# Dividing attention probabilities before the transposes in a fused block-attention and gMLP kernel

## The chip, the core and the metric

The kernel runs on one core of one Trainium2 chip. Five engines matter: TensorE (PE: matmuls and transposes into PSUM; PEld is its weight load), VectorE (DVE), ScalarE (ACT), GpSimd (POOL) and SyncE (SP), whose queue issues the kernel's loads and stores. Each engine works through its own queue in order and waits on semaphores. The metric is device microseconds of one execution; a time below is the median of several executions, and one further execution was profiled.

## The reference, cut to what matters

```python
# attention: q, k, v are (8, 8, 576, 64) f32; the mask lets block i see blocks j <= i, blocks of 64
scores = q @ k.T / 8;  scores = where(mask, scores, -1e9)
attn = exp(scores - scores.max(-1));  attn = attn / (attn.sum(-1) + 1e-9)
x = (attn @ v) -> (8, 576, 512)          # heads side by side
# gMLP: d_ff = 1024
h = gelu_tanh(x @ w_in);  u, v = halves of h
v_n = (v - mean) / sqrt(var + 1e-6) * g_ln
gated = u * (w_sg @ v_n + b_sg[:, None])
out = x + gated @ w_out
```

## The kernel before, in words

**Precision.** Matrix products whose operands must keep float32 accuracy are split: an operand is copied into a rounded high part (`fp32r`) and the rest is subtracted into a low part, and three products (high·high, low·high, high·low) are accumulated. So q and k, x, the normalised v, the gated values and all weights each need a copy and a subtraction. `w_in` and `w_out` arrive as float64 and are turned into float32 by one ScalarE pass and three DVE passes per 128x256 chunk (`from_f64`), ahead of their split.

**Attention, in slots.** A pair is two heads of one batch element; there are 32, four per batch element. `slot(n)` finishes pair n (its values, class `Values`) while it starts pair n+1 (its scores, class `Scores`). The 576 query rows stand in five tiles of rows: tile 0 has 64, tiles 1 to 4 have 128 each, and tile i needs 64+128·i key columns. On PE a slot runs `turn0` (transposes of the first 128 probability columns of tiles 4, 3, 2, 1, for head a=0, then 1), step 1 (scores of tile 4, first half, and tile 1), `av0`, `turn2`, step 2 (tile 4, second half), `turn1`, `turn_first`, step 3 (tiles 3 and 0), `av2`, step 4 (tile 2), `av1`, `av00`. Behind each step DVE takes the maximum (`maximum`, a custom instruction and a one-element read of its accumulator), and ScalarE the exponential with the row sum as an accumulator (`exponent`).

**Normalisation before.** Probabilities are not divided. `inverse` (line 438) forms 1/(sum+1e-9) on DVE and GpSimd spreads it into `rx`, 128x640; `turn_sums` (line 456) sends `rx` through PE with five transposes per slot; `normalise` (line 487) copies the accumulated output to `x` on ScalarE and multiplies it by the transposed sums on DVE. `x` is stored to DRAM (`spill`) and `split` into `xh` and `xl` for the feed-forward part.

**Feed-forward, in holes.** After four slots a batch element's `v_part` (5 pieces of PE work), `u_part` (8), the previous element's `o_part` (8) and its own `s_part` (8) are queued. Each slot has seven places called `hole`, and the strings in `PLAN` (in `FIRST` for slots 4 to 7) tell how many pieces each place takes. In slots 0 to 3 the queue is empty, so these slots hold attention alone. LayerNorm runs as small pieces (`moments`, `centre`, `scale`) taken from a list at fixed places; `WS` tells how many weight chunks a slot asks for.

**What sets the order.** PE instructions keep program order (`PIN = "P"`). For the other engines and for SP's queue the compiler's scheduler chooses the order: it takes instructions as its own model of time makes them ready, so code order there is only a starting point. Once chosen, each engine's order is fixed.

## Time and profile before

| | |
|---|---|
| time, median of 3 | 837.57 us (836.84 to 838.59) |
| profiled execution | 838.82 us, span of its instructions 836.9 us |
| mean granted TensorE clock | 0.966 |
| bytes moved | 65.67 MB, mean 78 GB/s |
| chain that ended last | PE 63%, DVE 20%, ACT 6%, DMA 5%, POOL 3%, issue 3% |

Busy time of one engine is a share of the whole span; what limits the kernel differs by stage: a start of some 26 us, attention alone up to 77 us, the first batch element with feed-forward work up to about 190 us, a regular part with one batch element per 97 to 99 us up to 767 us, and feed-forward alone to the end. A row of a timeline gives start, duration, what ran, and in brackets the idle time of the engine before it and what ended it. A row of the windows gives each engine's busy time (and instructions) in one stretch. A row of the groups gives total busy time, mean ns of one instruction and the idle time ahead of them.

### The profile page before, as it was taken

To read this page: it belongs to the slowest core of one execution; us is meant where nothing else is said; L and a number is where in the kernel's file an instruction comes from. 1 tells how busy PE (TensorE), PEld (TensorE's weight loads), DVE (VectorE), ACT (ScalarE), POOL (GpSimd) and SP (SyncE) were. 2 spreads that over 40 slices of the span, in tenths; PEclk is the share of its full clock that TensorE was granted. 3 is DMA by queue.
4 is the path that set the end of the run, shared out by engine and by line. 5 is a ranking of instruction groups with operands and counts; after the bars stand their busy time and mean duration, and the time that the engine had idled before them with its cause. 6 is when DMAs were issued, how large, how long until landed. Compare 5 with 4: busy or idle time off the path is not lost.

```text
span 836.9 us, 15898 instructions
## 1 busy us (share of the span) xinstructions
PE 788.5 (94%) x5926; PEld 649.0 (78%) x5926; DVE 531.6 (64%) x1504; ACT 424.4 (51%) x1124; POOL 352.7 (42%) x402
## 2 busy tenths in 40 slices
PE   5798992999999999999999999999999999999998
PEld 3466871878878888887887878788787878878998
DVE  6876474894865658564776747766586647753432
ACT  4776663656654367344653357642764446531400
POOL 5445158461543417432372513634164323713251
PEclk8799995999999999999999999999999999999999
DMA  7233205221122112310133101321123201230031
GB/s 251 77 114 115 85 18 159 80 61 57 44 86 99 58 58 72 126 59 30 58 108 120 58 28 31 126 101 57 58 71 122 77 16 57 75 112 29 1 114 71
DMA packets 46912, 65.67 MB, mean 78 GB/s; under 512 B 4082, under 2 KB 22514, under 8 KB 46836
## 3 DMA queue, kind: packets, MB, share of 16 engines
q1 hardware_dynamic: 46836, 64.67, 24.1%
q8 instruction: 46, 0.75, 0.4%
q14 instruction: 30, 0.25, 0.1%
HBM read 45.78 MB, written 18.87 MB: 77 GB/s over the span
## 4 chain that ended last, share of the span: by engine, by line
PE 63%; DVE 20%; ACT 6%; DMA 5%; POOL 3%; issue 3%; SPq 0%; DVEq 0%; ACTq 0%; POOLq 0%
PE accs L86 14%; PE accv L86 13%; PE acco L86 9%; PE ob L86 9%; PE s L86 7%; PE pb L89 3%; DVE prob L99 3%; DVE bs L99 3%; DVE vh L99 2%; DVE vv L99 2%; PE pa L89 2%; PE accu L86 2%; ACT prob L99 2%; PE pc L89 2%; DMA xr<-spill 2%
## 5 line engine op out<-in xcount | busy, mean ns | idle before, releaser
L99 ACT ACTIVATE prob<-prob,negm 128x448 f32<-128x448 f32 (+3 forms) x320 | 178.0, 558 | 157.8 <-DVE negm L99 154.1
L99 DVE CUSTOM_DVE_ANT_0 prob<-s,mask 128x288 f32<-128x288 f32 (+2 forms) x320 | 119.4, 421 | 37.2 <-PE s L86 36.5
L99 POOL TENSOR_TENSOR q_l<-q_f,q_h 128x576 fp32r<-128x576 f32 x31 | 44.2, 1425 | 196.1 <-PE s L86 158.3
L86 PE MATMUL ob<-pt,v_f 128*64 128x512 f32 (+4 forms) x640 | 115.3, 452 | 0.0
L99 POOL TENSOR_TENSOR gl<-u,gh 128x288 fp32r<-128x288 f32 x64 | 52.3, 824 | 105.1 <-DVE gh L99 72.9
L86 PE MATMUL accs<-ws_h,vh 128*128 128x288 f32 x256 | 79.8, 312 | 8.9 <-DVE vh L99 8.9
L86 PE MATMUL s<-k_h,q_h 64*128 64x288 f32 (+1 forms) x372 | 86.7, 351 | 1.2 <-DVE negm L99 1.2
L86 PE MATMUL accs<-ws_h,vl 128*128 128x288 f32 x256 | 76.8, 300 | 6.1 <-POOL vl L99 6.1
L86 PE MATMUL accu<-xh,wi_h 128*128 128x288 f32 x256 | 78.6, 307 | 1.3 <-ACT wi_h L99 1.3
L86 PE MATMUL acco<-gh,wo_h 128*128 128x288 f32 x256 | 79.8, 312 | 0.0
L86 PE MATMUL acco<-gl,wo_h 128*128 128x288 f32 x256 | 76.5, 299 | 0.0
L86 PE MATMUL acco<-gh,wo_l 128*128 128x288 f32 x256 | 76.4, 299 | 0.0
L86 PE MATMUL accs<-ws_l,vh 128*128 128x288 f32 x256 | 76.2, 298 | 0.0
L86 PE MATMUL accu<-xh,wi_l 128*128 128x288 f32 x256 | 75.4, 295 | 0.3 <-POOL wi_l L99 0.3
L86 PE MATMUL accu<-xl,wi_h 128*128 128x288 f32 x256 | 75.6, 295 | 0.0
L86 PE MATMUL s<-k_l,q_h 64*128 64x288 f32 (+1 forms) x372 | 72.2, 298 | 0.0
L86 PEld LDWEIGHTS ob<-pt,v_f 128*64 128x64 f32 x640 | 40.1, 139 | 40.9 <-issue 20.8
L86 PE MATMUL accv<-wi_h,xh 128*128 128x512 f32 x160 | 66.2, 414 | 0.7 <-POOL xh L99 0.7
L99 DVE TENSOR_TENSOR xr<-acco,xr 128x288 f32<-128x288 f32 x64 | 29.0, 454 | 59.2 <-PE acco L86 21.7
L86 PE MATMUL s<-k_h,q_l 64*128 64x288 f32 (+1 forms) x372 | 66.1, 293 | 0.0
L99 DVE TENSOR_TENSOR u<-accs,u 128x288 f32<-128x288 f32 x64 | 28.7, 448 | 57.6 <-PE accs L86 57.6
L86 PEld LDWEIGHTS s<-k_h,q_h 64*128 64x128 f32 x372 | 49.6, 180 | 18.2 <-issue 12.4
(106 smaller groups left out, 2109.9 us busy)
## 6 DMA issues: line engine op xcount, KB each, us to landing
spill<-x SPq DMA_DIRECT2D x32, 288.0 KB, 3.0
xr<-spill SPq DMA_DIRECT2D x32, 288.0 KB, 3.1
out_T<-xr SPq DMA_DIRECT2D x32, 288.0 KB, 2.4
q_f<-in_qT SPq DMA_DIRECT2D x31, 288.0 KB, 3.1
k_f<-in_kT SPq DMA_DIRECT2D x31, 288.0 KB, 3.4
v_f<-in_v SPq DMA_DIRECT2D x32, 256.0 KB, 3.3
raw<-in_w_in SPq DMA_DIRECT2D x16, 256.0 KB, 5.0
raw<-in_w_out SPq DMA_DIRECT2D x8, 256.0 KB, 4.3
```

Of the source, the lines that this page charges most:

```text
L86: return pin(nc.tensor.matmul(*a, **k), "P")
L89: return pin(nc.tensor.transpose(out, in_, identity), "P")
L99: return lambda *a, **k: pin(f(*a, **k), self.letter)
```

## The change

The probabilities themselves are divided. `divide` runs behind the exponentials: two small DVE instructions form 1/(sum+1e-9) for one or two tiles, then tile 4 (576 columns) is multiplied on DVE and tile 3 (448) on GpSimd, by a two-tensor instruction whose second operand is the broadcast reciprocal, and tiles 0 to 2 on ScalarE with the reciprocal as scale. `inverse`, `turn_sums` and the two multiplications of `normalise` go, and with them the five transposes per slot. In LayerNorm, `scale` no longer uses GpSimd: ScalarE writes the scaled high part, one DVE instruction the low part. q and k are loaded into one tile and rounded by one DVE copy of 1152 columns. `WS` asks for the weights of `v_part` alone in the first four slots, `FIRST` moves the first s pieces to the end of slot 6, the start-up keeps DVE and ScalarE in program order, `xr` is loaded one piece ahead, and `split` of a batch element's first two pairs waits until its second slot ends.

```diff
-            q_f = sp.tile([P, S], F32, tag="q_f", name="q_f", bufs=1)
-            k_f = sp.tile([P, S], F32, tag="k_f", name="k_f", bufs=1)
+            t = sp.tile([P, 2, S], F32, tag="qk_f", name="qk_f", bufs=1)
+            q_f, k_f = t[:, 0, :], t[:, 1, :]
...
     def split_qk(n):
+        t = qk[n]
+        hi = sp.tile([P, 2, S], F32R, tag="qk_h", name="qk_h", bufs=1)
+        lo = sp.tile([P, 2, S], F32R, tag="qk_l", name="qk_l", bufs=1)
+        V.tensor_copy(hi, t)
+        for i in (1, 0):
+            G.tensor_tensor(lo[:, i, :], t[:, i, :], hi[:, i, :].bitcast(F32), op=ALU.subtract)
...
-        A.activation(m.bitcast(F32), hi.bitcast(F32), AF.Abs, scale=2.0**-112)
+        A.mul(m.bitcast(F32), hi.bitcast(F32), 2.0**-112)
...
+        def divide(self, *tiles):
+            i0, i1 = min(tiles), max(tiles)
+            ts = slice(i0, i1 + 1, max(i1 - i0, 1))
+            V.tensor_tensor(self.ri[:, ts, :], self.sm[:, ts, :], tiny[:, ts, :], op=ALU.add)
+            V.reciprocal(self.ri[:, ts, :], self.ri[:, ts, :])
+            for i in tiles:
+                r, e = slice(0, QN[i]), EXT[i]
+                for a in (0, 1):
+                    x, c = self.prob[a][i][r, :e], self.ri[r, i, a : a + 1]
+                    if i < 3:
+                        A.mul(x, x, c)
+                    else:
+                        engine = V if i == 4 else G
+                        engine.tensor_tensor(x, x, c.broadcast_to([QN[i], e]), op=ALU.mult)
...
-            turn(self.t4[:, 128:256], self.rx[:, 0, :], ident)
-            t = self.rp = pbank("pe")
-            for i in range(1, NT):
-                turn(t[:, (i - 1) * P : i * P], self.rx[:, i, :], ident)
...
-            V.tensor_tensor(x[:, BLK:], self.rp, x[:, BLK:], op=ALU.mult)
-            V.tensor_tensor(x[:, :BLK], self.t4[:, 128:192], x[:, :BLK], op=ALU.mult)
...
-            paced(G.tensor_tensor(x, x, r.broadcast_to([rows, DH]), op=ALU.mult), "G")
             if st < NT - 1:
                 hi, lo = vn[st] = page(F32R, DH, "vh"), page(F32R, DH, "vl")
-                V.tensor_copy(hi, x)
-                G.tensor_tensor(lo, x, hi.bitcast(F32), op=ALU.subtract)
+                A.mul(hi, x, r)
...
+            paced(V.scalar_tensor_tensor(
+                lo, x, r, hi.bitcast(F32), op0=ALU.mult, op1=ALU.subtract
+            ), "V")
...
+        def reload(mo):
+            if mo < NC:
+                x_r[mo] = page(F32, S, "xr")
+                SP.dma_start(x_r[mo], spill.pop((b, mo)))
...
-    WS = [2, 2, 2, 2, 4, 3, 4, 4, 3]
+    WS = [2, 2, 2, 1, 10, 3, 3, 3, 2]
...
-    FIRST = ["1111111", "1111111", "1010101", "1010010"]
+    FIRST = ["1111111", "1111110", "0000011", "1111110"]
...
         if nx:
             nx.exponents(4)
+            nx.divide(4, 1)
...
             nx.exponents(3, 0)
+            nx.divide(3, 0)
             nx.step4()
         va.av1()
         va.av00()
-        va.turn_sums()
         if nx:
             nx.exponents(2)
+            nx.divide(2)
...
+    kept.update("VA")
     sc = Scores(0)
...
+    kept.difference_update("VA")
```

Three places of the instruction order bear on what follows. A number behind a tile's name is that of its buffer.

GpSimd, in slot 1, the second of the slots with attention alone (`q_l`, `k_l`, `qk_l`: low parts of q and k of the pair after next; `rx`: spread reciprocals; `xh`, `xl`: split of the finished pair's output; `prob_3`: tile 3 of the two heads of the next pair). Before:

```order
L99 TENSOR_TENSOR q_l<-q_f,q_h 128x576
L99 TENSOR_TENSOR k_l<-k_f,k_h 128x576
L99 MEMSET sums 128x2
L99 COPY rx<-ri 128x640
L99 TENSOR_TENSOR xh<-x,xh 128x64
L99 TENSOR_TENSOR xl<-x,xh 128x576
```

and with the change:

```order
L101 TENSOR_TENSOR qk_l<-qk_f,qk_h 128x576 x2
L101 TENSOR_TENSOR xh<-x,xh 128x64
L101 TENSOR_TENSOR xl<-x,xh 128x576
L101 TENSOR_TENSOR prob_3_114<-prob_3_114,ri 128x448
L101 TENSOR_TENSOR prob_3_123<-prob_3_123,ri 128x448
L101 MEMSET sums 128x2
```

The two multiplications of tile 3 stand last, behind both low parts and both instructions of `split`; slots 2 and 3 have the same order.

DVE, at the end of the same slot, from the last maxima (`ISA`, tile 2) to the copy that follows `turn0` (`pt<-pa`). Before:

```order
L99 ISA prob_2_110,negm<-s,mask 128x320
L99 ISA negm 128x1
L99 ISA prob_2_119,negm<-s,mask 128x320
L99 ISA negm 128x1
L99 CAST k_h<-k_f 128x576
L99 TENSOR_TENSOR x<-pe,x 128x512
L99 TENSOR_SCALAR ri<-sums 128x10
L99 TENSOR_TENSOR x<-pd,x 128x64
L99 RECIPROCAL ri<-ri 128x10
L99 CAST xh<-x 128x576
L99 COPY pt<-pa 128x512
```

and with the change:

```order
L101 ISA prob_2_112,negm<-s,mask 128x320
L101 ISA negm 128x1
L101 TENSOR_TENSOR prob_4_116<-prob_4_116,ri 128x576
L101 TENSOR_TENSOR prob_4_125<-prob_4_125,ri 128x576
L101 ISA prob_2_121,negm<-s,mask 128x320
L101 ISA negm 128x1
L101 CAST qk_h<-qk_f 128x1152
L101 TENSOR_TENSOR ri<-sums,tiny 128x2x2
L101 CAST xh<-x 128x576
L101 RECIPROCAL ri<-ri 128x2x2
L101 TENSOR_TENSOR ri<-sums,tiny 128x2
L101 RECIPROCAL ri<-ri 128x2
```

The multiplications of tile 4 stand between the two maxima of tile 2, and the reciprocal that tile 3's multiplication waits for stands behind the cast of q and k and the cast of `xh`.

SP's queue around the loads for the first `s_part` (`w_sgT`, `b_sg`). Before:

```order
L99 DMA w<-in_w_sgT 128x576 x2
L99 DMA v_f_103<-in_v 64x128
L99 DMA v_f_103<-in_v 128x4x128
L99 DMA q_f<-in_qT 128x576
L99 DMA spill<-x 128x576
L99 DMA w<-in_w_sgT 128x576 x2
L99 DMA w<-in_w_sgT 64x576 x2
L99 DMA raw<-in_w_out 128x256 x4
L99 DMA k_f<-in_kT 128x576
L99 DMA w<-in_b_sg 1x576 x2
```

and with the change:

```order
L101 DMA w<-in_w_sgT 128x576
L101 DMA w<-in_w_sgT 64x576 x2
L101 DMA w<-in_b_sg 1x576 x2
L101 DMA v_f_105<-in_v 64x128
L101 DMA v_f_105<-in_v 128x4x128
L101 DMA raw<-in_w_out 128x256 x2
L101 DMA spill<-x 128x576
L101 DMA raw<-in_w_out 128x256 x4
```

The bias `b_sg` stood behind a `spill` and four chunks of `w_out`; now it stands ahead of the values, the `spill` and all of `w_out`, and three of the four full `w_sgT` loads are issued earlier still, around the end of slot 0.

## The prediction

> **What bounds the kernel now.** I read the engine shares first, then windows by stage.

> ```profile
> span 836.9 us, 15898 instructions
> PE 788.5 (94%) x5926; PEld 649.0 (78%) x5926; DVE 531.6 (64%) x1504; ACT 424.4 (51%) x1124; POOL 352.7 (42%) x402
> ```

> ```profile
> 64.40:75.85 11.45, 10.33 (x95) 6.97 (x95) 8.90 (x33) 8.52 (x28) 5.33 (x7) 1.00 0.32 104
> 72.74:78.63 5.89, 4.77 (x38) 3.40 (x37) 4.99 (x16) 4.66 (x18) 3.90 (x5) 1.00 0.36 120
> 80.40:190.30 109.90, 92.47 (x668) 73.06 (x666) 73.64 (x208) 62.11 (x162) 55.87 (x58) 0.89 0.25 77
> 190.30:836.90 646.60, 634.88 (x4811) 535.96 (x4810) 396.87 (x1089) 309.32 (x801) 255.89 (x268) 0.99 0.22 71
> 484.40:581.40 97.00, 95.89 (x741) 79.59 (x741) 64.00 (x179) 50.88 (x134) 40.70 (x43) 1.00 0.23 74
> ```

> A window's row gives its length, then busy time of PE, PEld, DVE, ACT and POOL, the clock and DMA. PE is the bound nearly everywhere: in a regular batch element it is busy for 95.89 of 97.00 us, DVE for 64, ScalarE for 51, GpSimd for 41. A slot with attention alone takes 11.45 us with PE busy for 10.33. The first element with feed-forward work (80.4 to 190.3) holds 17.4 us of PE idle. PE's timeline shows what it waits for, with one row of DVE between:

> ```profile
> 13.07 3.83 PE L86 MATMUL s<-w 64*128 64x448 f32 x10 [4.87 <-DVE negm L99]
> 21.26 0.47 PE L89 MATMUL pa<-ident,prob 128*128 128x128 f32 x1 [3.96 <-ACT prob L99]
> 27.50 2.81 PE L86 MATMUL ob<-pt,v_f 128*64 128x512 f32 x4
> 43.96 1.24 PE L86 MATMUL ob<-pt,v_f 128*64 128x512 f32 x4
> 133.86 0.61 PE L86 MATMUL accs<-ws_h,vl 128*128 128x288 f32 x1 [4.65 <-POOL vl L99]
> 136.07 2.06 DVE L99 TENSOR_TENSOR ws_l<-w,ws_l 1x576 fp32r<-1x576 f32 x1 [7.42 <-ACT ws_l L99]
> 140.49 0.58 PE L86 MATMUL accs<-ws_h,vh 128*128 128x288 f32 x1 [5.78 <-DVE vh L99]
> ```

> and the list of waits (engine, waited for, total, times, longest):

> ```profile
> PE pd L89 <- DVE pt L99: 6.9, 6, 1.5
> ```

> At the start PE waits for maxima and exponentials; near 130 us DVE stands 7.42 us behind the bias of `w_sg` and PE waits for LayerNorm; later `pt` is late once per batch element. `av0` (the `ob` rows) begins slot 0's second part at 27.50 and slot 1's at 43.96.

> **The five transposes** go.

> ```profile
> 74.51 0.33 PE L89 MATMUL pd<-ident,rx 128*128 128x128 f32 x1
> 74.67 0.60 PE L89 MATMUL pe<-ident,rx 128*128 128x128 f32 x4
> 75.11 0.38 PE L89 MATMUL pa<-ident,prob 128*128 128x128 f32 x2
> ```

> From 74.51 to the next work at 75.11 they take 0.60 us. In the PE-bound slots 8 to 31 that is 24 x 0.60 = 14.4 us, if the division stays under PE. Room is there: per regular element ScalarE gains six multiplications a slot and LayerNorm's six, some 30 at 0.39 us or a little more (its copy of 288 columns, below), 12 us on 51. DVE gains two passes and six tiny instructions a slot and loses two multiplications, the sums and LayerNorm's casts: about even on 64. GpSimd loses LayerNorm's nine instructions and four `rx`, and gains eight multiplications: less than 41. The chain behind step 4 is covered by three to four pieces of feed-forward work before the next `turn0`. Where there are none, it is bare.

> **Slots 1 to 3, attention alone.** The durations, from the groups:

> ```profile
> L99 POOL TENSOR_TENSOR k_l<-k_f,k_h 128x576 fp32r<-128x576 f32 x31 | 45.5, 1469 | 9.9 <-DVE k_h L99 9.5 <-DVE ri L99 0.4
> L99 POOL TENSOR_TENSOR xl<-x,xh 128x576 fp32r<-128x576 f32 x32 | 45.4, 1418 | 0.1
> L99 POOL TENSOR_TENSOR xh<-x,xh 128x64 fp32r<-128x64 f32 x32 | 11.6, 361 | 2.4 <-DVE xh L99 2.2
> L99 POOL TENSOR_TENSOR vv<-vv,rs 128x512 f32<-128x512 f32 x32 | 35.8, 1118 | 0.0
> L99 DVE SCALAR_TENSOR_TENSOR vv<-vv,stats,g_bc 128x512 f32<-128x512 f32 x32 | 22.3, 740 | 0.0
> L99 DVE CUSTOM_DVE_ANT_0 prob<-s,mask 128x320 f32<-128x320 f32 x64 | 28.8, 484 | 0.2
> L99 DVE CAST q_h<-q_f 128x576 fp32r<-128x576 f32 x31 | 14.1, 456 | 33.1 <-issue 22.4 <-DMA q_f<-in_qT 6.9 <-PE s L86 3.8
> L99 DVE CAST k_h<-k_f 128x576 fp32r<-128x576 f32 x31 | 34.6, 1115 | 0.3 <-DMA k_f<-in_kT 0.3
> L99 DVE TENSOR_SCALAR ri<-sums 128x10 f32<-128x10 f32 x32 | 28.9, 903 | 0.9 <-ACT prob L99 0.9
> L99 ACT COPY u<-accu 128x288 f32<-128x288 f32 x64 | 23.9, 387 | 13.0 <-PE accu L86 12.8
> ```

> Estimates for what is new: tile 3's GpSimd multiplication 1118 x 448/512 = 0.98 us; tile 4's DVE pass 740 x 576/512 = 0.83; the cast of 1152 columns between 0.75 (part of q_h's 456 ns is fixed) and 0.91. By the new orders, from step 4's start: its products 0.65, a maximum 0.48, two passes 1.66, a maximum 0.48, the cast 0.75, so GpSimd starts at 4.0. Then, first in, first out: k and q low 2.9, `xh` 0.36, `xl` 1.42, tile 3 twice 1.96, together 10.6. The last transposes (0.4) and step 1 (0.95) end at 12.0, where the window 72.74:78.63, from step 4's start to step 1's end, shows 5.89. PE has its own work done some 2.4 us after step 4's start and then waits over 7 us inside `turn0`; everything of the next slot queues behind it. Lower bound: instructions overlap at their ends by about a tenth, 11.1, so +5.2. Upper: DVE also waits for GpSimd once, half an instruction, 0.7, so +6.7. I take +5.8, between them; three slots **+17.4** (15.6 to 20).

> The rows show DVE waiting out GpSimd: 903 ns for ten elements, 1115 against 456 ns for the same cast. [...]

> **The clock.** A wait of PE has an after-effect:

> ```profile
> 243.37 0.30 PE L89 MATMUL pd<-ident,prob 64*64 64x64 f32 x2 [1.53 <-DVE pt L99]
> 246.92 0.45 PE L86 MATMUL acco<-gl,wo_h 128*128 128x288 f32 x1
> 248.35 0.30 PE L86 MATMUL acco<-gl,wo_h 128*128 128x288 f32 x1
> ```

> After 1.53 us of waiting the same matmul takes 0.45 us, and 1.4 us later 0.30. The slow stretch from 243.5 to 248.1 is 4.6 us at two thirds of the speed: 1.5 us lost. For the waits in slots 1 to 3: **+4.5** (0 to +6). [...]

> **The start.** DVE and ScalarE now run the first scores in program order, without weights between.

> ```profile
> 9.51 1.32 DVE L99 TENSOR_SCALAR w<-raw 128x256 uint32<-128x256 uint32 x1 [0.31 <-DMA raw<-in_w_in]
> 12.28 0.45 DVE L99 CUSTOM_DVE_ANT_0 prob<-s,mask 128x288 f32<-128x288 f32 x1
> L99 DVE SCALAR_TENSOR_TENSOR w<-raw,w 128x256 uint32<-128x256 uint32 x24 | 14.0, 591 | 0.2
> L99 DVE TENSOR_SCALAR w<-raw 128x256 uint32<-128x256 uint32 x24 | 11.1, 467 | 0.3 <-DMA raw<-in_w_in 0.3
> L99 DVE SCALAR_TENSOR_TENSOR w<-w 128x256 uint32<-128x256 uint32 x24 | 10.8, 455 | 0.4 <-ACT w L99 0.3
> ```

> The first maximum can start near 7 instead of 12.28, and behind it stand some 10 us of maxima, passes and waits for exponentials; the cast of q and k then ends near 18, both low parts (2.9) near 21, and slot 0's `av0` comes there instead of at 27.50. That gain is not kept: the new order does not spread the weights. All 16 chunks of `w_in` (48 passes) stand on DVE between the cast of q and k, near 18 us, and slot 1's `turn0`. By the rows they take 16 x (0.59 + 0.47 + 0.46) = 24 us, and slot 0's maxima, copies and divisions some 12: slot 1's `av0` at 54. Those means hold waits; at 0.3 to 0.4 us a pass it is some 7 less, 47. It stood at 43.96; I take 50, the middle: **+6** (+3 to +10).

> **Slots 4 to 7.** A regular element has eight o pieces more; the chain of waits shows one:

> ```profile
> 429.34 1.60 PE acco L86 x12
> ```

> so without them 97.0 - 12.8 = 84.2 us, where 109.9 stand. The 25.7 of excess (weights late, `b_sg`, LayerNorm) goes: the first s piece moves to the end of slot 6 and `b_sg` is loaded ahead of `w_out`. The transposes give 2.4. New: in slot 5 GpSimd splits two pairs ahead of tile 3, so the chain ends near 14 us after step 4's start, while PE has work to 5.4: +8.5. At the ends of slots 6 and 7 two or three pieces cover most of it, +3.3; clock +2.5. Net **-13.8** (-20 to -6).

> **Slots 8 to the end.** Transposes -14.4. The 6.9 us of waits for `pt` stood behind loads of `xr`, which are now issued a piece ahead: -5.5, and the slow stretches after three of them -4.5. New waits, where low parts precede tile 3 on GpSimd: +2. Net **-22.4** (-27 to -13).

> The other edits (`mul` for `abs`, `tiny`, the short reciprocals) keep shapes or lie under PE. Sum: 6 + 17.4 + 4.5 - 13.8 - 22.4 = **-8.3**. The profiled execution's 838.82 becomes 830.5; it lies 1.25 above the median, whose 837.57 becomes **829.3**.

> **Rivals.** (1) *The chain does not bind*: tile 3 is done early and slots 1 to 3 stay at 11.5; 837.6 + 3 - 20 - 24 = **797**. For it: four chains of waits go at once. Against: GpSimd's order is fixed. (2) *Slower*: DVE and GpSimd wait for each other several times inside that chain and the slow clock lasts from slot 1 to 4: 11 us per slot instead of 5.8 + 1.5, and +10 at the start, 829.3 + 11 + 4 = **844**; with that start it decides from 9 us per slot. [...] Against: in these slots GpSimd is idle more than half of the time (5.33 of 11.45). (3) *No change*: in the covered slots, too, tile 3 comes late, by 0.35 us in each of 24: **838**. Against: 41 us of GpSimd work in 97.

> **Chances.** Forecast 0.50, (1) 0.17, (2) 0.23, (3) 0.10. The forecast's own terms reach from 815 to 841; with half of (1) and most of (2) the range is 808 to 846. Some 0.2% (1.7 us) can be told from no change: faster 0.65, same 0.11, slower 0.24.

> **What would show it.** Right: slots 1 to 3 at 17 to 19 us, PE's wait in them ended by GpSimd's `prob` at `pa`; no wait of PE for `vl` or `vh`; 94 instead of 97 us per element. Wrong: these slots near 12 us (1) or over 20 (2); elements still at 97 (3); slot 1's `av0` far from 50.

## The result: 22.6 us slower

The changed kernel takes **859.80 us** (859.01 to 862.54), the kernel before beside it 837.21: ratio **1.0284** (95% interval 1.0242 to 1.0326). The forecast was 829.3, faster.

The head of the page after, then windows of the profiled executions of before (first four rows) and after (last four), each cut at the `av0` of slots 0, 1, 4 and 8 and at the end:

```profile
span 857.2 us, 15851 instructions
PE 770.4 (90%) x5766; PEld 632.8 (74%) x5766; DVE 575.7 (67%) x1585; ACT 520.8 (61%) x1364; POOL 318.0 (37%) x363
```

```profile
27.50:43.96 16.46, 13.82 (x98) 8.05 (x96) 14.19 (x46) 11.06 (x34) 10.43 (x13) 0.82 0.09 25
43.96:80.39 36.43, 33.07 (x296) 22.50 (x294) 26.94 (x101) 26.21 (x82) 17.82 (x21) 1.00 0.38 121
80.39:185.82 105.43, 88.00 (x647) 70.09 (x645) 71.80 (x200) 61.01 (x158) 55.35 (x58) 0.89 0.26 80
185.82:836.90 651.08, 639.36 (x4834) 538.94 (x4832) 398.72 (x1098) 310.42 (x805) 256.40 (x269) 0.99 0.22 70
```

```profile
22.89:57.75 34.86, 15.48 (x92) 9.85 (x90) 30.71 (x80) 22.03 (x65) 24.67 (x25) 0.65 0.43 137
57.75:117.48 59.73, 38.00 (x280) 25.28 (x278) 32.87 (x109) 33.44 (x100) 21.60 (x24) 0.77 0.19 60
117.48:216.65 99.17, 85.30 (x627) 65.93 (x625) 78.17 (x204) 69.38 (x181) 43.83 (x47) 0.95 0.24 76
216.65:857.20 640.55, 619.06 (x4714) 522.75 (x4712) 422.25 (x1155) 384.73 (x987) 219.22 (x231) 1.00 0.22 71
```

PE is busy 18 us less (788.5 to 770.4) and the span is 20.3 us longer. By stage: slot 1's `av0` comes at 57.75 instead of 43.96 (+13.8), slots 1 to 3 take +23.3, slots 4 to 7 -6.3, the rest -10.5. The forecast had +6, +21.9, -13.8 and -22.4 there. Waits of PE after the change that were not there before, from its timeline:

```profile
49.63 0.45 PE L91 MATMUL pa<-ident,prob 128*128 128x128 f32 x1 [10.49 <-DVE prob L101]
54.43 1.79 PE L91 MATMUL pa<-ident,prob 128*128 128x128 f32 x7 [4.35 <-POOL prob L101]
74.27 1.79 PE L91 MATMUL pa<-ident,prob 128*128 128x128 f32 x7 [6.98 <-POOL prob L101]
112.30 1.79 PE L91 MATMUL pa<-ident,prob 128*128 128x128 f32 x7 [7.00 <-POOL prob L101]
168.93 1.97 PE L91 MATMUL pa<-ident,prob 128*128 128x128 f32 x7 [7.89 <-POOL prob L101]
264.03 0.33 PE L91 MATMUL pa<-ident,prob 128*128 128x128 f32 x1 [1.79 <-POOL prob L101]
265.27 1.17 PE L91 MATMUL pa<-ident,prob 128*128 128x128 f32 x6 [0.91 <-ACT prob L101]
```

All of these stand at `pa`, in `turn0`, and wait for a divided tile: tile 4 (DVE), then tile 3 (GpSimd), then tile 2 or 1 (ScalarE). Slot 3's `turn0`, not shown, has the same wait of 7.00 us. The last two rows are the first of six such places, one in each batch element from the third on, always where the element's third pair begins. One regular element:

```profile
461.52:557.23 95.71, 92.85 (x723) 77.20 (x721) 68.16 (x189) 62.92 (x164) 36.24 (x39) 1.00 0.23 76
```

It took 97.0 us with PE busy for 95.89; now PE is busy 3.0 us less, and 1.3 us of that arrive.

### The profile page after: what moved, and what is told of

It reads as the page before. It is cut to its first block, busy times and chain, and to the rows that moved or that the text cites. A ratio compares the mean times of both kernels' runs of the same rounds, so it can differ in the third digit from the quotient of the medians.

```text
span 857.2 us, 15851 instructions
## 1 busy us (share of the span) xinstructions
PE 770.4 (90%) x5766; PEld 632.8 (74%) x5766; DVE 575.7 (67%) x1585; ACT 520.8 (61%) x1364; POOL 318.0 (37%) x363
## 4 chain that ended last, share of the span: by engine, by line
PE 58%; ACT 17%; DVE 13%; issue 3%; POOL 2%; ACTq 0%; DVEq 0%
PE accs L88 13%; PE acco L88 11%; PE accv L88 10%; ACT prob L101 8%; PE s L88 7%; PE ob L88 7%; PE pb L91 3%; PE pa L91 3%; DVE prob L101 2%; DVE bs L101 2%; PE pc L91 2%; ACT L101 2%; ACT vh L101 2%; DVE ri L101 2%; DVE vv L101 2%
## 5 line engine op out<-in xcount | busy, mean ns | idle before, releaser
L101 ACT ACTIVATE prob<-prob,negm 128x448 f32<-128x448 f32 (+4 forms) x320 | 177.6, 557 | 99.3 <-DVE negm L101 95.1
L101 DVE CUSTOM_DVE_ANT_0 prob<-s,mask 128x288 f32<-128x288 f32 (+2 forms) x320 | 119.1, 420 | 29.6 <-PE s L88 28.9
L101 POOL TENSOR_TENSOR prob<-prob,ri 128x448 f32<-128x448 f32 x64 | 66.5, 1059 | 190.7 <-DVE ri L101 190.7
L101 POOL TENSOR_TENSOR qk_l<-qk_f,qk_h 128x576 fp32r<-128x576 f32 x62 | 93.9, 1536 | 105.2 <-PE accu L88 60.7
L88 PE MATMUL ob<-pt,v_f 128*64 128x512 f32 (+4 forms) x640 | 112.5, 450 | 2.3 <-DVE pt L101 2.3
L91 PE MATMUL pa<-ident,prob 128*128 128x128 f32 x256 | 43.7, 305 | 71.7 <-POOL prob L101 49.9
L101 ACT ACTIVATE prob<-prob,ri 128x192 f32<-128x192 f32 (+2 forms) x192 | 77.8, 451 | 39.2 <-DVE ri L101 39.2
L91 PEld LDWEIGHTS pa<-ident,prob 128*128 128x128 f32 x256 | 32.2, 153 | 78.9 <-POOL prob L101 53.2
L88 PE MATMUL s<-qk_h 64*128 64x288 f32 (+1 forms) x372 | 86.7, 356 | 1.9 <-DVE negm L101 1.3
L101 DVE TENSOR_TENSOR ri<-sums,tiny 128x4 f32<-128x4 f32 (+1 forms) x96 | 42.0, 437 | 47.5 <-ACT prob L101 45.9
L88 PE MATMUL s<-qk_l,qk_h 64*128 64x288 f32 (+1 forms) x372 | 72.3, 301 | 0.0
```

What stands on the lines that cost most here:

```text
L88: return pin(nc.tensor.matmul(*a, **k), "P")
L91: return pin(nc.tensor.transpose(out, in_, identity), "P")
L101: return lambda *a, **k: pin(f(*a, **k), self.letter)
```

## The experiments

Thirteen kernels, each run beside the kernel before. Every edit also lets the scheduler choose other orders on DVE, ScalarE and GpSimd; no run holds these fixed, so a difference between two runs is that of the edit and of the orders that came with it. The four columns on the right are from the profiled executions: slot 1's `av0`, and the lengths of the stages as above.

| run | time, us | ratio to before (interval) | slot 1's av0 | slots 1–3 | slots 4–7 | 8 to end |
|---|---|---|---|---|---|---|
| before | 837.2 | | 43.96 | 36.43 | 105.43 | 651.08 |
| changed | 859.80 | 1.028 (1.024–1.033) | 57.75 | 59.73 | 99.17 | 640.55 |
| e6 changed, no division | 795.01 | 0.950 (0.947–0.953) | 47.73 | 39.65 | 89.42 | 615.80 |
| e5 before, no normalisation | 807.08 | 0.965 (0.962–0.968) | 43.59 | 35.41 | 102.37 | 623.83 |
| e4 before, new plan | 835.51 | 0.9975 (0.9961–0.9989) | 48.69 | 37.63 | 100.37 | 647.91 |
| e3 changed, old plan | 865.27 | 1.034 (1.031–1.038) | 56.75 | 55.88 | 111.06 | 638.71 |
| e1 tile 3 first | 851.63 | 1.018 (1.015–1.021) | 56.58 | 54.31 | 98.28 | 640.13 |
| e2 tile 3 on ScalarE | 867.95 | 1.037 (1.033–1.041) | 58.98 | 55.40 | 95.80 | 656.92 |
| e10 gelus behind tile 2 | 863.78 | 1.032 (1.029–1.034) | 57.84 | 59.45 | 101.59 | 643.62 |
| e7 e1 and e10 | 844.76 | 1.010 (1.007–1.012) | 56.20 | 54.11 | 98.78 | 633.41 |
| e8 pairs 0–3 as before | 836.69 | 1.0003 (0.9985–1.0022) | 47.86 | 45.62 | 99.80 | 641.62 |
| e9 e7 and e8 | 823.85 | 0.985 (0.981–0.989) | 47.24 | 43.07 | 96.29 | 633.70 |
| e11 division where covered | **806.55** | **0.964 (0.961–0.967)** | 47.43 | 39.30 | 95.71 | 622.16 |
| e12 e11 and e1 | 806.48 | 0.964 (0.961–0.967) | 46.98 | 40.74 | 94.50 | 621.98 |
| e13 e11, old start-up | 809.47 | 0.968 (0.965–0.971) | 49.76 | 40.66 | 96.65 | 620.43 |

### What the division costs, and what it replaces: e6, e5

```diff
# e6: the changed kernel
         def divide(self, *tiles):
+            return
# e5: the kernel before
-        va.inverse()
...
-            turn(self.t4[:, 128:256], self.rx[:, 0, :], ident)
-            t = self.rp = pbank("pe")
-            for i in range(1, NT):
-                turn(t[:, (i - 1) * P : i * P], self.rx[:, i, :], ident)
...
-            V.tensor_tensor(x[:, BLK:], self.rp, x[:, BLK:], op=ALU.mult)
-            V.tensor_tensor(x[:, :BLK], self.t4[:, 128:192], x[:, :BLK], op=ALU.mult)
```

> The changed kernel without the division: no sums plus tiny, no reciprocals, no multiplications on ScalarE, DVE and GpSimd, so that the probabilities stay unnormalised; LayerNorm, plan and the missing transposes stay. Theory A (all of the loss hangs on the division): slots 1 to 3 at 10.8 to 11.5 us (-25 in all), no wait at the end of slot 5 (-8 to -10), regular elements at 93 to 94 us instead of 95.7 (-2 x 6 = -12), the start some 4 to 8 us earlier: 803 to 812 us. Rival (plan and LayerNorm carry a good part): 825 us or more.

> The kernel before without its normalisation: no reciprocals of the sums, no spreading on GpSimd, no five transposes a slot, no two multiplications of the output, so that the output stays unnormalised; the plan, LayerNorm and everything else as before. It prices what the change takes away. Prediction: 0.60 us a slot, 32 x 0.60 = 19 us, nothing else, 817 to 820 us. Rival (the reciprocals, the spreading and the multiplications also stood in the way of pt's copies, whose waits of about 1.2 us per element with their slow stretch go too): regular elements of 93 us or less instead of 97, 808 to 814 us.

Windows of one regular element, e6 first, then e5, and of e6's first and last stage:

```profile
361.33:453.39 92.06, 91.92 (x722) 76.92 (x720) 53.63 (x158) 54.36 (x140) 27.89 (x30) 1.00 0.24 78
```

```profile
368.20:461.37 93.17, 92.99 (x723) 77.34 (x721) 57.77 (x164) 50.94 (x134) 37.94 (x39) 1.00 0.25 77
```

```profile
16.55:47.73 31.18, 15.82 (x93) 9.87 (x91) 24.93 (x73) 19.95 (x59) 22.76 (x21) 0.66 0.43 135
176.80:792.60 615.80, 611.38 (x4714) 519.71 (x4712) 339.29 (x971) 335.38 (x849) 171.75 (x185) 1.00 0.23 74
```

Without the division the changed kernel takes 795.0, so the division costs 64.8 us and the rest of the change gains 42. The cost by stage, changed minus e6: start 10.0, slots 1 to 3 20.1, slots 4 to 7 9.75, slots 8 to end 24.75. The first theory had 803 to 812: right in kind, and still 8 us short of what the division costs.

The old normalisation cost 30 us (837.05 to 807.08), 11 more than its five transposes at 0.60 us in 32 slots: the rival for e5 held, and was itself a little low in its gain. In a regular element 3.8 us go, where four slots' transposes are 2.4; PE's waits for `pt` are gone too. `xr` is loaded by the same code and DVE still waits for it, but less long: 2.60 us in the third batch element instead of 4.41. Its load is issued 2.7 us earlier in the slot (2.23 instead of 4.95 us after `av0` of slot 10).

### The plan: e4, e3, e13

```diff
# e4 (in the kernel before) and e3 (back, in the changed one); start-up likewise
-    WS = [2, 2, 2, 2, 4, 3, 4, 4, 3]
+    WS = [2, 2, 2, 1, 10, 3, 3, 3, 2]
-    FIRST = ["1111111", "1111111", "1010101", "1010010"]
+    FIRST = ["1111111", "1111110", "0000011", "1111110"]
# e13: e11, start-up of before, slot 4's share 8 instead of 10
-    kept.update("VA")
     sc = Scores(0)
     sc.step1()
...
     sc.exponents(4)
+    weight_step()
```

> The kernel before with the new plan alone: the new shares of weights, the new holes of slots 4 to 7, the new start-up with DVE and ScalarE in program order. Nothing is divided, LayerNorm is the old one. By the prediction's terms the plan costs the start some 4 (the run without division has slot 1's av0 at 47.73 where before has 43.96) and takes the wait for b_sg and LayerNorm near 130 us away, 10 to 18 us of slots 4 to 7: 822 to 832 us. Rival (the stall is only moved: the weights of w_out come later and are waited for): 835 us or more.

> The changed kernel with the loading plan of before: the old shares of weights per slot, the old holes in slots 4 to 7, the old start-up (weights between the first scores, DVE and ScalarE not pinned). Theory A (the start's loss comes from all of w_in's chunks standing in slots 0 and 1): av0 of slot 1 comes at 44 to 49 us instead of 57.75, slots 1 to 3 keep their 18 to 20 us, and the stall for b_sg and LayerNorm near 130 us returns (some 15 to 20 us in slots 4 to 7): 858 to 866 us. Rival (the division itself makes the start late): av0 of slot 1 stays at 54 or later, and the time is 870 us or more.

> The run with the division in covered slots only, with the start-up of before: four chunks of weights between the first pair's scores, DVE and ScalarE not pinned there, and slot 4's share 8 instead of 10. It tells which part of the plan makes the start later. If it is the start-up's order, av0 of slot 1 comes at 44 to 45 us instead of 47.43 and all later slots 2 to 4 us earlier: 802.5 to 804.5 us. If it is the shares per slot (all of w_in's v chunks in slots 0 to 3 in both), the time stays within 1.5 us of 806.5.

The plan alone gains 2 us: it costs 4.7 at the start, and the stall near 130 us is moved rather than removed. e4's timeline of PE:

```profile
142.33 1.20 PE L91 MATMUL pc<-ident,prob 128*128 128x128 f32 x4 [3.77 <-DVE pt L101]
153.02 0.40 PE L88 MATMUL accs<-ws_h,vh 128*128 128x288 f32 x1 [2.12 <-DVE vh L101]
157.17 0.61 PE L88 MATMUL accs<-ws_h,vl 128*128 128x288 f32 x1 [3.75 <-POOL vl L101]
```

LayerNorm's `vh` and `vl` are still late there; in the changed kernel, with GpSimd out of LayerNorm, no PE wait for them of 0.2 us or more is left. In e3 the old plan brings the stall back (slots 4 to 7 at 111), but slot 1's `av0` stays at 56.75. Its time, 865.27, lies in the range of theory A, which its start refutes: the right time for the wrong reason. The division makes the start 10 us later with the new plan (changed against e6) and 13 with the old one (e3 against e5, which differ in the change's smaller edits too), the plan only 4 to 5 without division (e6 against e5, again with the smaller edits, and e4 against before). e13 speaks against the new start-up order as the source of these 4 to 5: with the old one in e11, slot 1 begins later still (49.76), and its 809.47 us met neither of its forecasts. Whether they come from the shares of weights in slots 0 to 3 stays open.

### Two queues, not one: e1, e2, e10, e7

```diff
# e1: GpSimd's low parts behind tile 3 (split_qk; split likewise)
-        for i in (1, 0):
-            G.tensor_tensor(lo[:, i, :], t[:, i, :], hi[:, i, :].bitcast(F32), op=ALU.subtract)
+        with tc.issue_after(tile3[0]):
+            for i in (1, 0):
+                G.tensor_tensor(lo[:, i, :], t[:, i, :], hi[:, i, :].bitcast(F32), op=ALU.subtract)
# e2: tile 3 on ScalarE
-                    if i < 3:
+                    if i < 4:
# e10: gelus behind tile 2
-            with tc.issue_after(after):
+            with tc.issue_after(after), tc.issue_after(tile2[0]):
# e7: e1 and e10
```

> The changed kernel with one more rule: on GpSimd the low parts of q, k and x are issued behind tile 3's two multiplications of the same slot, instead of ahead of them. Theory A (the order of GpSimd's queue makes the loss): tile 3 no longer stands behind q and k low (2.97 us), xh and xl (1.7 us); step 1 still waits for the low parts, now 1.9 us later than tile 3. Slots 1 to 3 (19.85, 18.57, 21.31 us) get 2 to 3 us shorter each, the wait at the end of slot 5 (7.89 us) shrinks to about 3, the wait of 1.79 us for GpSimd's prob once per later element goes (6 x 1.8 = 11 us) while the one of 0.95 us for ScalarE's prob behind it may stay: 837 to 843 us. Theory B (DVE and GpSimd exclude each other, whatever the order): slots 1 to 3 stay within 0.5 us, the later waits stay, 856 us or more.

> The changed kernel with tile 3's two multiplications on ScalarE instead of GpSimd, nothing else. Theory A (queue order on GpSimd): about the gain of the run with tile 3 first, or a little more, since GpSimd then has 1.9 us less in front of step 1: 835 to 842 us; slots 1 to 3 at 16 us. Theory B (DVE and GpSimd exclude each other): a gain of the same size here, where nothing is gained by reordering alone. Theory C (ScalarE becomes the late one: exponentials and six to eight multiplications in its queue, 0.4 to 0.5 us each): the wait per element only changes its releaser from GpSimd to ScalarE and the time stays within 5 us of 859.8.

> The changed kernel with one more rule: each batch element's gelus on ScalarE are issued behind tile 2's two multiplications that were asked for last (in the run with tile 3 first, a table load of 1.28 us and two to three gelus stood ahead of them). GpSimd's order stays. Theory C (two chains are late at once, tile 3 on GpSimd and tile 2 on ScalarE, and PE waits for the later one): once per regular element the 0.95 us wait for ScalarE's prob goes and the 1.79 us for GpSimd's stays, so elements of 94.7 instead of 95.7 us; slot 5's 7.89 us stays: 852 to 856 us. Theory A (GpSimd's order alone): 858 us or more.

> Both rules at once: low parts behind tile 3 on GpSimd, gelus behind tile 2 on ScalarE. Theory C (two chains): now the wait once per element goes whole (2.75 to 3 us and the slow stretch behind it), elements come to 92.5 to 93.5 us, near the 92.05 of the run without division, which is 14 to 19 us over six of them; slot 5's last wait (5.35 us with tile 3 first) falls below 2.5: 826 to 835 us. Rival (the division delays every tile through DVE's and ScalarE's fuller queues, whatever the gelus): less than 5 us below the 851.6 of tile 3 first.

e1 gains 8 us, of which 5.4 lie in slots 1 to 3, and next to nothing in the later elements; its time lies between the two theories' ranges. GpSimd's order as the whole cause falls: the wait there only changes its owner. PE's timeline in e1, slots 2 to 3 and 13 to 14:

```profile
86.98 0.33 PE L91 MATMUL pa<-ident,prob 128*128 128x128 f32 x1 [3.40 <-POOL prob L101]
89.26 1.54 PE L91 MATMUL pa<-ident,prob 128*128 128x128 f32 x6 [1.95 <-ACT prob L101]
354.92 0.89 PE L91 MATMUL pa<-ident,prob 128*128 128x128 f32 x6 [2.96 <-ACT prob L101]
```

The other chain ends in tile 2. The changed kernel's timeline at the same place, DVE, GpSimd and ScalarE:

```profile
357.05 3.32 DVE L101 CAST xh<-x 128x576 fp32r<-128x576 f32 x2
360.29 0.89 DVE L101 TENSOR_TENSOR ri<-sums,tiny 128x2 f32<-128x2 f32 x1
```

```profile
356.99 3.06 POOL L101 TENSOR_TENSOR qk_l<-qk_f,qk_h 128x576 fp32r<-128x576 f32 x2 [9.43 <-PE accu L88]
359.99 2.06 POOL L101 TENSOR_TENSOR prob<-prob,ri 128x448 f32<-128x448 f32 x2
```

```profile
359.44 1.28 ACT L101 ACT_TABLE_LOAD   x1
360.73 1.25 ACT L101 ACTIVATE u<-u 128x576 f32<-128x576 f32 x2
361.89 1.00 ACT L101 ACTIVATE prob<-prob,ri 128x320 f32<-128x320 f32 x2
```

Tile 2's exponentials are done at 357.7 (its second one's sum). Then its reciprocal stands behind two casts on DVE, and its multiplications behind a table load and two gelus on ScalarE, so they begin 4 us later. The two casts are those of `split`: the change puts it off for an element's first two pairs until the second slot ends, which is just this place. No run moved them alone. Tile 3 ends on GpSimd at 362.05, tile 2 on ScalarE at 362.89: two chains, late within a microsecond of each other, so that mending one only uncovers the other. With tile 3 moved to ScalarE (e2), that engine's queue grows, PE waits 4.1 us per element for it, and the time grows by 8 us, more than the 5 that theory C allowed. With the gelus moved alone (e10) tile 3's 1.79 us stays, as forecast, but the forecast time of 852 to 856 was missed: the median is 4 us higher instead, about as much as the changed kernel's own runs differ. With both (e7) 15 us are gained in all, 7 of them beyond e1, where 17 to 26 had been expected:

```profile
350.24 0.89 PE L91 MATMUL pa<-ident,prob 128*128 128x128 f32 x6 [0.79 <-ACT prob L101]
354.88 1.08 PE L88 MATMUL ob<-pt,v_f 128*64 128x512 f32 x4 [1.25 <-ACT pt L101]
```

The second row is new: `pt` is now the one behind four gelus. The same new wait of 1.24 to 1.25 us stands in two of e10's elements. In the four others, no such wait stands, but PE's granted clock falls to 0.50 for 3.4 us behind `turn0`, which in the changed kernel it does in one element alone: there e10's loss in the later elements is slow clock, not a wait (the last section comes back to it).

### The division only where PE has work beside it: e8, e9, e11, e12

```diff
# e8: pairs 0 to 3 keep inverse, turn_sums and the two multiplications of before
         def divide(self, *tiles):
+            if self.n < 4:
+                return
...
+        if n < 4:
+            va.inverse()
# e9: e7 and e8. e11: this condition instead of n < 4. e12: e11 and e1
+    def old(n):
+        return n < 5 or n % 4 == 2
```

> The changed kernel in which the first batch element's four pairs, whose slots have little or no feed-forward work beside them, are normalised as before (the sums' five transposes and two multiplications of the output), and the other 28 pairs by division. Theory (the loss at the start and in slots 1 to 3 is the bare chain of the division): av0 of slot 1 at 47 to 50 us as without division (47.73), slots 1 to 3 at 38 to 42 us in all instead of 59.73, everything from slot 4 on as in the changed kernel (99 and 640): 826 to 833 us. Rival (the plan's weights in slot 0 make the start late): av0 of slot 1 stays at 55 or later, 837 us or more.

> The changed kernel with the first four pairs normalised as before, low parts behind tile 3 on GpSimd, and gelus behind tile 2 on ScalarE. If the gains add: 836.7 (the first alone) minus 859.8 - 844.8 = 15 (the other two), of which some 5 lay in slots 1 to 3 and are not there twice: 825 to 828 us. If they don't, because both shorten the same waits: 832 or more.

> The changed kernel with the division only where PE has work to cover its chain: pairs 0 to 4 and every pair whose slot's start showed the wait (the third of each batch element) are normalised as before, the other 21 pairs by division; no order is changed. Theory (the loss is the bare chain at these places, everywhere else the division lies under PE): the 5.2 us wait at the end of slot 3, the 7.9 at the end of slot 5 and the 2.75 us per later element go, each for one slot's five transposes (0.6 us): 836.7 - 5 - 7 - 6 x 2.7 = 806 to 814 us, regular elements at 92.5 to 93.5. Rival (the wait moves to the next pair's start, as it moved from GpSimd to ScalarE with tile 3 first): 825 us or more.

> As the run with the division in covered slots only, with GpSimd's low parts behind tile 3 as well. If tile 3 is late nowhere any more, within 2 us of that run; if what is left of the waits is tile 3's, 2 to 6 us less.

In e8 slot 1's `av0` comes at 47.86, as without division, and slots 1 to 3 are 14 us shorter; what is left there is a 5.17 us wait at the end of slot 3, where pair 4, the first divided one, is uncovered. The start's loss was the division's, not the weights'; the forecast for e8, 826 to 833, forgot that last wait. In e9 the gains add, as forecast; it comes out 1 us below the 825 to 828 named.

e11 takes the old way for pairs 0 to 4 and for the third pair of each batch element, where the long waits in `turn0` stood, the new way at the 20 others (the 21 in the expectation is miscounted), and adds no rule of order. Shorter waits stay where they are divided, the longest 1.36 us at the start of slot 8. With e12, which is equal to it within noise, it is the fastest version that leaves nothing out, 30 us below before and 53 below the changed kernel. Its regular element:

```profile
323.87:416.70 92.83, 92.53 (x725) 77.52 (x725) 63.44 (x186) 60.69 (x159) 35.02 (x38) 1.00 0.24 78
```

PE is idle for 0.30 us of it, a wait for `pt`. The element is 0.8 us above e6's, about the 0.6 us of one slot's transposes. With that, tile 3's order makes no difference any more (e12).

## Why the prediction was wrong

**Slots 1 to 3: right, and by the mechanism named.** Forecast +17.4 and +4.5 for the clock, measured +23.3; PE's waits "over 7 us" ended by GpSimd's `prob` are 6.98, 7.00 and 7.00, and the clock is 0.77. In slot 1 GpSimd starts 3.8 us after step 4 (forecast 4.0), and its chain ends at 10.2 (forecast 10.6):

```profile
64.92 0.42 PE L88 MATMUL s<-qk_h 64*128 64x320 f32 x2
68.72 2.97 POOL L101 TENSOR_TENSOR qk_l<-qk_f,qk_h 128x576 fp32r<-128x576 f32 x2 [8.66 <-issue]
73.28 1.82 POOL L101 TENSOR_TENSOR prob<-prob,ri 128x448 f32<-128x448 f32 x2
```

The cast of 1152 columns took 0.76 us there (forecast 0.75). The tenth of overlap in the lower bound lies between what before shows: DVE's instructions last 621.3 us added up and keep it busy for 531.6, GpSimd's 362.6 and 352.7, so 14% and 3% overlap. Run e1 shows what the forecast's chain left out: behind tile 3 a second one, tile 2's on ScalarE, was only 1.8 us shorter per slot (54.31 against 59.73 for three).

**The start: the term was mis-sized**, +6 against +13.8, outside its bounds of 3 to 10. Of its two sums the upper one, 54, held as far as it went: the cast of q and k starts at 17.92, all 48 weight passes then take 23.5 us (forecast 24), and all else on DVE, the division included, takes 10.7 ("some 12"). Two steps failed. The lower sum, 0.3 to 0.4 us a pass, with which the middle of 50 was taken, did not come about: the shortest passes take 0.28 and 0.41 us, but the 48 took 0.49 on average. And the sum stopped at DVE. DVE's last reciprocal ends at 52.97; tile 3 on GpSimd, the rest of `turn0` and step 1 follow, and `av0` comes 4.8 us later:

```profile
52.82 0.15 DVE L101 RECIPROCAL ri<-ri 128x2 f32<-128x2 f32 x1
53.45 1.82 POOL L101 TENSOR_TENSOR prob<-prob,ri 128x448 f32<-128x448 f32 x2
```

Without the division the plan alone costs 3.8 us here (e6, with the change's smaller edits) or 4.7 (e4). The division adds work to DVE where it is already busy for 24.93 of 31.18 us (e6; 30.71 of 34.86 with it), and PE's longest wait of all, 10.49 us, is for tile 4's pass.

**Slots 4 to 7: mis-sized on both sides**, -13.8 against -6.3. "The 25.7 of excess goes": from `av0` to `av0` the stage held only 105.4 - 84.2 = 21.2, and without division the change takes 16.0 off it. The wait at the end of slot 5 came as forecast (8.5, measured 7.89), and the stage's cost of the division was 9.75, less than the 14.3 forecast (8.5, 3.3 and 2.5).

**Slots 8 to the end: here the sign was lost.** The gain was even underrated: -24.4 forecast for transposes, `pt` and clock, -27.3 measured in e5 for the normalisation alone, -35.3 in e6 for the whole change without division. The cause given for `pt`, the loads of `xr`, agrees with the rows of before:

```profile
242.25 0.46 DVE L99 TENSOR_TENSOR xr<-acco,xr 128x288 f32<-128x288 f32 x1 [4.41 <-DMA xr<-spill]
242.63 0.68 DVE L99 COPY pt<-pb 128x512 f32<-128x512 f32 x1
```

It was not the only way to be rid of them: they stay in e4, which has the old loads and the old normalisation, and go in e5, where only the normalisation is out and the load comes earlier in the slot. The failed step is "New waits, where low parts precede tile 3 on GpSimd: +2"; it measured 24.75. Of these 17 are idle time of PE (21.5 against 4.4 us) and 7.7 longer busy time (619.06 against 611.38), which was not traced to a cause. The forecast looked at one queue, GpSimd's, and at one cover, "three to four pieces of feed-forward work before the next `turn0`". It did not ask what else stands in ScalarE's and DVE's queues ahead of the division: where `u` ends, a table load and gelus on ScalarE and the two late casts of `split` on DVE, and `turn0` now needs something that stands behind them; in e6, where it needs the exponentials alone, no wait of 0.2 us or more is left there.

**The clock.** The rule behind the clock terms was read from one place in before, with a slow stretch from 243.5 to 248.1. By the granted clock it begins at 244.9, 1.5 us after the wait ended, and lasts 3.4 us:

```profile
243.40:244.90 1.50, 1.50 (x16) 1.26 (x18) 1.25 (x6) 1.12 (x3) 0.00 (x0) 1.00 0.00 0
244.95:248.25 3.30, 3.30 (x15) 2.22 (x12) 1.31 (x8) 3.30 (x12) 0.00 (x0) 0.50 0.23 89
```

**The range** was too narrow by its own terms: their bounds, added up, reach from 809 to 855, where 815 to 841 was written. The measured 859.8 lies outside even these.

**The rivals.** The slower one (844) named DVE and GpSimd waiting for each other in slots 1 to 3, deciding from 9 us per slot, and +10 at the start; no run shows the 11 us per slot of its sum: it was 7.8 per slot with the clock in it and +13.8 at the start, so its side was right and, but for the start, its place wrong. The third (tile 3 late in covered slots, 0.35 us in each of 24) was nearest: it is late in one slot of four, by 2.75 us together with tile 2. That the chain does not bind is excluded.

**DVE beside GpSimd.** The prediction read DVE's long rows as waits for GpSimd and counted one of them, half an instruction long, for its upper bound. The rows after agree with that at this place: `ri` on two columns takes 0.89 us and ends at 361.18, when GpSimd's first multiplication ends (359.99 + 1.17 = 361.16), and the mean of this form, 946 ns, is five times that of the `ri` on four columns (183 ns):

```profile
L101 DVE TENSOR_TENSOR ri<-sums,tiny 128x2 f32<-128x2 f32 x32 | 30.3, 946 | 8.2 <-ACT prob L101 7.4
L101 DVE TENSOR_TENSOR ri<-sums,tiny 128x4 f32<-128x4 f32 x64 | 11.7, 183 | 39.3 <-ACT prob L101 38.5
```

How much of the 64.8 us these waits of DVE make was not measured by itself; in e1, whose edit concerns GpSimd alone, DVE is busy for 413.85 instead of 422.25 us from slot 8 on.

## What to carry to other kernels

Work that moves from behind a result to in front of it costs its latency through every queue it passes, not its busy time: follow the moved value through each engine that handles it (here sum, DVE, then ScalarE or GpSimd) and read what stands ahead of it in each queue at the place where cover is thinnest. Two chains that end within a microsecond of each other have to be shortened together, or avoided. And where a cheaper form pays only under cover, choose per place: 20 pairs one way and 12 the other took 3.6% less than the kernel before and 6% less than the changed one.

## What the runs showed of the hardware that was not expected

The slow clock does not follow from the length of PE's wait alone. In the kernel before, matmuls were slow after a wait of 1.53 us. In e2 they are slow after each of six waits of 4.08 to 4.10 us. In e1 six waits of 2.96 to 2.99 us stand at the same place of six elements; matmuls run at full speed after five of them and are slow after the first:

```profile
257.69 1.27 PE L91 MATMUL pa<-ident,prob 128*128 128x128 f32 x6 [2.99 <-ACT prob L101]
```

```profile
450.60 0.89 PE L91 MATMUL pa<-ident,prob 128*128 128x128 f32 x6 [2.99 <-ACT prob L101]
451.47 0.30 PE L88 MATMUL acco<-gl,wo_h 128*128 128x288 f32 x1
```

```profile
653.96 1.54 PE L91 MATMUL pa<-ident,prob 128*128 128x128 f32 x6 [4.08 <-ACT prob L101]
656.02 0.44 PE L88 MATMUL acco<-gh,wo_h 128*128 128x288 f32 x1
```

```profile
254.61:258.02 3.41, 0.42 (x4) 0.33 (x4) 3.39 (x4) 3.38 (x7) 3.41 (x3) 1.00 0.00 1
258.02:261.43 3.41, 3.41 (x18) 3.41 (x15) 0.99 (x2) 2.97 (x5) 3.41 (x4) 0.50 0.68 191
445.76:449.17 3.41, 1.85 (x15) 1.62 (x13) 3.38 (x4) 3.38 (x8) 3.41 (x4) 1.00 0.18 69
449.17:452.58 3.41, 1.98 (x16) 1.95 (x17) 2.75 (x4) 3.41 (x7) 3.41 (x3) 1.00 0.23 51
```

From slot 8 on, the changed kernel has two full-speed steps in which PE was idle for more than 1.82 us: 2.65 us (262.29 to 265.70) and 2.53 us (852.79 to 856.20). The clock was 0.50 behind both, and behind no other. The waits at the next of its six places are spread over two steps, 1.82 and 0.95 us (357.86 to 364.68), and the clock stayed at 1.00, as it did in e1 behind 1.56 and 1.43 us, where 2.99 us in one step were followed by a slow one. So in these two runs it counted, too, where a wait fell among the steps; whether e10's four slow stretches come from that was not shown. In the kernel before, steps with 1.53, 1.27 and 0.99 us of idle time (from 241.50, 340.49 and 439.47) were followed by slow ones; why less was enough there stays open.

In e2 the slow clock makes an element of 98 to 99 us out of a 4.1 us wait: beside e6's 92.06, it costs 2 to 3 us more.
